# A gated long convolution and SwiGLU block: split norm statistics, a last stage in 64-row pairs, two spectra kept in SBUF, and a third weight buffer

## Chip, cores and metric

The kernel runs on one core of a Trainium2 chip. The metric is the device time of one execution in microseconds (us), the median of five runs. The profiler records a single execution, whose span is counted from its first to its last recorded work; that execution's own time is given beside it.

## What is computed

One block of an adaLN-conditioned model on a sequence of 2048 rows of width 576, in bf16. Six rows `sa, ca, ga, sb, cb, gb` come from a condition vector. The first half is a gated long convolution, the second half a SwiGLU of width 4608:

```python
h = _layernorm(x) * (1 + ca) + sa
# k_shift: 4-tap causal filter over the rows of k
kv = k_shift * v
y = irfft(rfft(kv, 2 * S) * rfft(ssm_k, 2 * S))[:S] + kv * ssm_D
x = x + ga * (h * y)
h = _layernorm(x) * (1 + cb) + sb
x = x + gb * ((silu(h @ w1) * (h @ w3)) @ w2)
```

## The kernel before

**Blocks.** The convolution is done over 8 blocks of 256 rows (`s` = 0 to 7). Each block of `kv` has a spectrum `X[s]` and each block of the filter has a spectrum `W[s]`, from which `V[s]` is made of two neighbours; both are [128, 6, 576] bf16, 0.885 MB. Block s of the result is the sum over j of `X[j] * V[s - j]` (`pair`, L400 to L412: two VectorE operations, a product and a sum, per term), put back by `inverse` (L539, TensorE), and joined to x in `residual` (L552 to L554, VectorE). Spectra that later blocks need are written to HBM by `keep_x` (L417) and `keep_v` (L421) and read back by `get` (L433) into `spec`, a pool of three buffers for X and four for V; `old_x` and `old_v` say which are still in SBUF.

**Statistics.** A norm's sums are made by ScalarE (`ln_sums`, L440: a copy and a square with an accumulated output). `ln_scales` (L455 to L460) makes mean, variance, `pow(var, -0.5)` and the shift of them in six GpSimd operations on 128x2 values. For the first norm the result is used by `gate_rows` (L500, ScalarE, tile `hg`), for the second by `normed_act` (L566, ScalarE, tile `h2row`). Block 0 and 1 use VectorE's batch-norm instructions in part (`quick_stats`, L470 to L473).

**Turns.** `turn_all(s)` transposes `h2row` on TensorE (L571), and ScalarE writes it scaled to `h2T` (L601), the input of the SwiGLU.

**Stages.** `row_blocks` runs four stages r of 512 rows. `stream` makes the hidden rows of 36 chunks ("items") of 128 columns. An item fills two PSUM banks, one for w1 and one for w3. As 576 is 4.5 times 128, each bank gets four full 128-row matmuls (`full`, L916, 128x512) and one of 64 rows (`rest`, L927); the two half ones of an item lie in the upper and lower half of the array. Items go in groups of 2, in the last stage of 4: the full ones of the early items, then all half ones, then the full ones of the late items. `hide` then applies Silu (L935) and copies the second bank (L937) on ScalarE and multiplies on VectorE (L938). `down` (L982) multiplies with w2: two halves of 288 columns, each with 144 matmuls of 128x288 and 9 w2 chunks loaded by SyncE, evicted at L999 and L1000.

**What sets the order.** The convolution of blocks 2r+2 and 2r+3 (`conv`, `outcome`, generators that yield a cost in us) is threaded through stage r: after each item and each w2 chunk `advance` runs steps until a budget is spent. The amounts are `CONV_US` over a time of 93.5 us. `behind(engine)` pins an instruction's place behind the last one already issued on that engine. `first_block` does block 0 in a hand-written order, `conv_second` block 1. The last stage has no convolution beside it. In `down`, at half 1, chunk 5, what is left of the convolution is run off and `turn_all(2r + 3)` issued. All weight and spectra transfers are issued by SyncE in program order.

**Weight buffers.** `wst` has three buffers of [128, 9, 512]. `load_w13` (L867, L868) brings a chunk of w1 and w3 (four items, 1.15 MB) into one of them. From stage 1 on, chunks alternate between buffers 0 and 1; `wst[2]` then serves `down` as four w2 buffers (`w2m`). Two lines of it, from `row_blocks` and `down`:

```python
jobs = [(fc, 0, RB, (r + fc) % 2, ...) for fc in range(NF // FC)]
w = _ap(self.w2m, (h * NF + f0) // W2C % NW2 * W2C * H, [[H, W2C], [1, H]])
```

Of the kernel before, what the change touches and what calls it, by code (L numbers as in the profile page):

```python
# [9 lines left out]
BF16 = mybir.dt.bfloat16  # L10
F32 = mybir.dt.float32
I32 = mybir.dt.int32
ALU = mybir.AluOpType
ACT = mybir.ActivationFunctionType

P = 128
# [16 lines left out]
N1 = 24  # L33
SPLIT = 2
EPS = 1e-5

# [7 lines left out]
class _Kernel:  # L44
    def __init__(self, ctx, tc, q, k, v, shift_k, ssm_k, ssm_D, w1, w3, w2, c, w_mod, out):
        self.tc, self.nc = tc, tc.nc
        self.q, self.k, self.v = q, k, v
        self.shift_k, self.ssm_k, self.ssm_D = shift_k, ssm_k, ssm_D
        self.w1, self.w3, self.w2, self.c, self.w_mod, self.out = w1, w3, w2, c, w_mod, out
        pool = lambda name, **kw: ctx.enter_context(tc.tile_pool(name=name, **kw))  # L50
        self.const = pool("const", bufs=1)
        self.psum = pool("psum", bufs=4, space=bass.MemoryType.PSUM)
        self.dram = pool("spill", bufs=1, space=bass.MemoryType.DRAM)
        self.spec = pool("spec", bufs=4)
        self.wprev = pool("wprev", bufs=2)
        self.prod = pool("prod", bufs=1)
        self.acc = pool("acc", bufs=1)
        self.ld = pool("ld", bufs=1)
        self.kvp = pool("kvp", bufs=1)
        self.x1p = pool("x1p", bufs=4)  # L60
        self.lnp = pool("lnp", bufs=1)
        self.small = pool("small", bufs=4)
        self.hp = pool("hp", bufs=4)
        self.xo, self.hg, self.accs, self.l1 = {}, {}, {}, {}
        self.X, self.V, self.Wl = {}, {}, {}
        self.w13, self.kept = {}, {}

    def ps(self, shape=(P, 2, 512), dtype=F32):
# [280 lines left out]
    def x_sums(self, s):  # L349
        X = self.X[s]  # L350
        self.nc.vector.tensor_add(X[:, 0:6:3, :], X[:, 1:6:3, :], X[:, 2:6:3, :])
        if 3 < s < NBLK - 2:
            self.keep_x(s)
        yield 0.75
# [68 lines left out]
    def old_x(self, i, s):  # L423

        return self.X[i] if s == 2 or s == 4 and i > 0 else self.get("X", i)

# [9 lines left out]
    def ln_sums(self, src, i, ssum, ssq, col=None):  # L436
        col = i if col is None else col
        for func, out in ((ACT.Copy, ssum), (ACT.Square, ssq)):
            junk = self.lnp.tile([P, D], BF16, name="junk", tag="junk")
            self.nc.scalar.activation(junk[:], src[:, i, :], func, accum_out=out[:, col:col + 1])  # L440

    def ln_stats(self, src, name):

        ssum = self.small.tile([P, 2], F32, name=name + "s", tag="ssum")
        ssq = self.small.tile([P, 2], F32, name=name + "q", tag="ssq")
        for i in range(2):
            self.ln_sums(src, i, ssum, ssq)
        return self.ln_scales(ssum, ssq, name)

    def ln_scales(self, ssum, ssq, name):  # L450
        small = self.small
        n = ssum.shape[-1]
        mean, var, rstd, nmr = [small.tile([P, n], F32, name=name + k, tag=f"ln{k}{n}") for k in "mvrn"]
        e = self.nc.gpsimd
        e.tensor_single_scalar(mean[:], ssum[:], -1.0 / D, op=ALU.mult)  # L455
        e.tensor_scalar(var[:], ssq[:], 1.0 / D, EPS, op0=ALU.mult, op1=ALU.add)
        e.tensor_mul(rstd[:], mean[:], mean[:])
        e.tensor_sub(var[:], var[:], rstd[:])
        e.tensor_tensor(rstd[:], var[:], self.neghalf[:, 0:n], op=ALU.pow)
        e.tensor_mul(nmr[:], mean[:], rstd[:])  # L460
        return rstd, nmr
# [22 lines left out]
    def gate_stats(self, s):  # L484

        ssum, ssq = [self.small.tile([P, 2], F32, name="l1" + k, tag=t) for k, t in (("s", "ssum"), ("q", "ssq"))]
        for i in range(2):
            with self.behind(self.nc.scalar):
                self.ln_sums(self.xo[s], i, ssum, ssq)
            yield 0.8  # L490
        self.l1[s] = self.ln_scales(ssum, ssq, "l1")

# [68 lines left out]

    def normed_act(self, s, r, b):
        row, x1 = self.h2row, self.xo[s]
        for cc in range(2):
            for lo, hi, at in ((0, D, 0), (512, D, D)):
# [62 lines left out]
    def first_block(self):  # L628
# [54 lines left out]
        self.ln_sums(x1, 0, sums[0], sums[1], 0)  # L683
        scales = [self.ln_scales(*sums, "l1"), (rstd, nmr)]
        for m in (1, 0):
# [50 lines left out]
    def outcome(self, s, fill, waits, between=None, quick=False):  # L736


        def steps():
# [19 lines left out]
            else:  # L759
                with self.behind(nc.scalar):  # L760
                    r, b = self.ln_stats(self.xo[s], "l2")
                yield -waits[2]
                with self.behind(nc.scalar):
                    self.normed_act(s, r, b)
            yield -waits[3]
# [11 lines left out]
    def conv_second(self):  # L777
        yield from self.gate_stats(1)
        yield from self.kv_rows(1)
        yield from self.v_block(1)  # L780
        yield from self.pair(self.X[0], self.V[1], 1)
        yield from self.x_spectrum(1)
        self.mod_piece(5)
# [9 lines left out]
    def conv(self, s0):  # L793
# [13 lines left out]
        def old():  # L807
            V, X = self.old_v(s0 - 1, s0), self.old_x(1, s0)
            yield from self.pair(X, V, s0)
            for j in range(2, s0):  # L810
                X = self.old_x(j, s0)
                yield from self.pair(X, V, s1)
                V = self.old_v(s0 - j, s0)
                yield from self.pair(X, V, s0)
            self.V1 = V
            yield from self.gate_stats(s0)
            yield from self.kv_rows(s0)
            if s0 == 2:
                yield from self.pair(self.X[0], self.V[s0], s0)
        yield from self.mix(filters(), old())  # L820
        self.gate_rows(s0)
        X0, V0 = self.old_x(0, s0), self.old_v(0, s0)

        def beside():
            yield from self.v_block(s1)
            with self.behind(self.nc.sync):
                self.load_kv(s1)
            yield from self.gate_stats(s1)
            if s0 > 2:
                yield from self.pair(X0, self.V[s0], s0)  # L830
            self.X1 = self.old_x(1, s0)
            yield from self.pair(X0, self.V[s1], s1)
            yield from self.gate(s0)
        yield from self.mix(self.x_spectrum(s0), beside())
# [7 lines left out]
        def others():  # L842
            yield from self.kv_rows(s1)
            yield from self.mix(self.x_spectrum(s1), more())
            yield from self.x_sums(s1)
# [35 lines left out]
    def stream(self, r, jobs, rate, size, finish=False):  # L881
# [49 lines left out]
        def hide(k):  # L931
# [7 lines left out]
            del gus[k]  # L939
            self.advance(rate * 2.05)  # L940

# [4 lines left out]
        for k in range(0, len(items), size):  # L946
# [13 lines left out]
            for m in late:  # L960
                full(m, False)
                hide(m)

    def down(self, r, rate):
# [71 lines left out]
    def row_blocks(self, n1):  # L1036
        for r in range(NRB):
# [17 lines left out]
            else:  # L1055
                spills = {1: (self.keep_x, 1), 2: (self.keep_v, 0), 4: (self.keep_v, 1)} if r == 1 else {}
                jobs = [(fc, 0, RB, (r + fc) % 2, (lambda f, i: lambda: f(i))(*spills[fc]) if fc in spills else None)
                        for fc in range(NF // FC)]
            self.stream(r, jobs, rate, 4 if r == NRB - 1 else 2)
            self.down(r, rate)  # L1060
# [54 lines left out]
```

## Time and profile before

| | |
|---|---|
| five runs, us | 517.81, 518.19, 518.25, 518.63, 519.36 |
| median | 518.25 |
| profiled execution, its own time | 518.19 |
| its span | 516.1 |
| TensorE matmul busy | 498.1 us, 97% |
| VectorE, ScalarE, GpSimd busy | 341.2, 292.8, 63.6 us |
| moved by DMA | 107.76 MB, 209 GB/s |
| L916, full matmuls | 1317 records, 263.7 us |
| L927, half matmuls | 336, 42.4 us |
| L982, `down` | 1152, 145.3 us |
| Xd written, read | 6 and 8 transfers of 864 KB |
| Vd written, read | 4 and 4 |

In the groups a line gives the code line, the engine, the operation and its tiles as output<-input, then the count, the busy time and the mean of one in ns. Durations of matmuls overlap, as they are pipelined; the distance from start to start is what counts. In the timeline a bracket holds the idle time of the engine ahead of a group and what ended it. In the chain, lines give start, length, engine, tile and line. The stages, by the first matmuls of each: stage 0 up to 163 us, stage 1 to 283, stage 2 to 399, the last from there to the end. The page's "PEclk" is the clock that TensorE was granted, in tenths of full speed.

### The profile page before, as it was taken

The numbers are of one execution on the slowest core, as the hardware profiler recorded it, in microseconds if no ns is written. First come the engines' busy times: TensorE is split into PE (matmuls) and PEld (weight loads), VectorE is DVE, ScalarE is ACT, GpSimd is POOL, SyncE is SP. The second block draws the span as 40 slices with busy tenths as digits, with TensorE's granted clock in tenths as the row PEclk, the third lists the DMA queues.
The fourth block names the chain that finished last, engine by engine and source line by source line (L and its number), as shares of the span: only waits on it lengthen the run. The fifth ranks groups of instructions, "written<-read, shape, count | busy, mean of one in ns | idle before, by whom it ended". The sixth has DMA issues, their size and how long they took to land.

```text
span 516.1 us, 8602 instructions
## 1 busy us (share of the span) xinstructions
PE 498.1 (97%) x3334; PEld 294.3 (57%) x3362; DVE 341.2 (66%) x515; ACT 292.8 (57%) x581; POOL 63.6 (12%) x109
## 2 busy tenths in 40 slices
PE   7999988999999999999998999999999999999997
PEld 3767763556787444344776543434588544444775
DVE  8899898999994364997999984299660212112012
ACT  5758697578443569659552465976806345445000
POOL 3303013104040001201017000120101000000000
PEclk9989998999999999999999999999999999999999
DMA  8947968587979857559999863645555553550462
GB/s 274 323 150 217 321 197 253 161 287 240 294 250 343 262 185 217 185 157 322 343 321 353 286 190 127 188 158 169 151 139 139 148 173 121 162 168 10 118 181 70
DMA packets 102204, 107.76 MB, mean 209 GB/s; under 512 B 5075, under 2 KB 94228, under 8 KB 102164
## 3 DMA queue, kind: packets, MB, share of 16 engines
q1 hardware_dynamic: 102142, 107.21, 66.5%
q8 instruction: 26, 0.43, 0.4%
q14 instruction: 14, 0.11, 0.1%
q10 hardware_dynamic: 22, 0.01, 0.0%
HBM read 96.00 MB, written 11.21 MB: 208 GB/s over the span
## 4 chain that ended last, share of the span: by engine, by line
PE 76%; DVE 13%; DMA 4%; ACT 3%; issue 2%; POOL 2%; SPq 0%; POOLq 0%; ACTq 0%
PE ps L916 38%; PE ps L982 24%; PE ps L927 6%; DMA wst<-in_B_w_dram 3%; DVE p L410 2%; PE ps L313 2%; PE ps L299 2%; PE ps L539 2%; DVE z L412 2%; DVE h L938 1%; DVE kv L335 1%; DVE kvt L334 1%; DMA knat<-in_A_ssm_k_dram 1%; PE ps L219 1%; PE ps L364 1%
## 5 line engine op out<-in xcount | busy, mean ns | idle before, releaser
L916 PE MATMUL ps<-h2T,wst 128*128 128x512 bf16 (+1 forms) x1317 | 263.7, 350 | 2.8 <-ACT W L315 0.8
L916 PEld LDWEIGHTS <-wst 128*128 128x128 bf16 x1344 | 127.9, 98 | 122.3 <-issue 19.5
L935 ACT ACTIVATE h<-ps 128x512 bf16<-128x512 f32 x144 | 87.0, 604 | 108.4 <-PE ps L927 70.8
L982 PE MATMUL ps<-wst,h 128*128 128x288 bf16 x1152 | 145.3, 286 | 3.1 <-DMA wst<-in_B_w_dram 2.4
L982 PEld LDWEIGHTS <-h 128*128 128x128 bf16 x1152 | 112.3, 98 | 32.7 <-issue 3.9
L938 DVE TENSOR_TENSOR h<-h,u 128x512 bf16<-128x512 bf16 x144 | 60.1, 420 | 96.1 <-ACT u L937 95.9
L937 ACT CAST u<-ps 128x512 bf16<-128x512 f32 x144 | 84.9, 590 | 0.0
L410 DVE TENSOR_TENSOR p<-X,V 128x3456 bf16<-128x3456 bf16 x28 | 54.6, 1949 | 5.7 <-DMA X<-Xd 5.5
L412 DVE TENSOR_TENSOR z<-z,p 128x3456 bf16<-128x3456 bf16 x28 | 54.6, 1950 | 0.2
L999 DVE TENSOR_TENSOR og<-ps,gbrow 128x288 bf16<-128x288 f32 x32 | 13.1, 448 | 48.9 <-PE ps L982 48.9
L927 PE MATMUL ps<-h2T,wst 64*128 64x512 bf16 (+1 forms) x336 | 42.4, 349 | 2.4 <-ACT X L315 2.1
L440 ACT ACTIVATE junk<-x 128x576 bf16<-128x576 bf16 x54 | 37.6, 696 | 0.5
L927 PEld LDWEIGHTS <-wst 64*128 64x128 bf16 x336 | 11.4, 94 | 29.4 <-issue 26.6
L455 POOL TENSOR_SCALAR l2m<-l2s 128x2 f32<-128x2 f32 x6 | 8.8, 1469 | 154.4 <-ACT junk L440 154.4
L601 ACT ACTIVATE h2T<-ps,sbcol,cbcol 128x256 bf16<-128x256 bf16 x35 | 16.7, 570 | 17.6 <-PE ps L571 17.6
L566 ACT ACTIVATE h2row<-x,l2n,l2r 128x576 bf16<-128x576 bf16 (+1 forms) x24 | 13.8, 654 | 21.2 <-POOL l2n L460 21.2
L455 POOL TENSOR_SCALAR l1m<-l1s 128x2 f32<-128x2 f32 x7 | 4.4, 634 | 131.6 <-ACT junk L440 131.6
L334 DVE TENSOR_TENSOR kvt<-kh,shk 128x1152 bf16<-128x1152 bf16 x24 | 18.0, 750 | 2.6 <-DMA kh<-in_A_k_dram 2.4
L335 DVE TENSOR_TENSOR kv<-kv,kvt 128x1152 bf16<-128x1152 bf16 x24 | 18.0, 752 | 0.3
L315 ACT CAST X<-ps 128x576 bf16<-128x576 f32 x24 | 15.5, 658 | 0.0
L745 ACT CAST y<-ps 128x576 bf16<-128x576 f32 x14 | 8.6, 653 | 11.1 <-PE ps L539 11.1
L405 DVE TENSOR_TENSOR z<-X,V 128x3456 bf16<-128x3456 bf16 x7 | 13.6, 1949 | 0.9 <-PE ps L927 0.9
(137 smaller groups left out, 370.2 us busy)
## 6 DMA issues: line engine op xcount, KB each, us to landing
wst<-in_B_w_dram SPq DMA_DIRECT2D x80, 512.0 KB, 4.8
wst<-in_B_w_dram SPq DMA_DIRECT2D x72, 288.0 KB, 3.8
X<-Xd SPq DMA_DIRECT2D x8, 864.0 KB, 5.5
Xd<-X SPq DMA_DIRECT2D x6, 864.0 KB, 5.9
wst<-in_B_w_dram SPq DMA_DIRECT2D x80, 64.0 KB, 3.0
kh<-in_A_k_dram SPq DMA_DIRECT2D x7, 720.0 KB, 7.7
Vd<-V SPq DMA_DIRECT2D x4, 864.0 KB
V<-Vd SPq DMA_DIRECT2D x4, 864.0 KB
```

Source lines behind the costliest of these rows:

```text
L334: nc.vector.tensor_mul(tmp[:], kh[:, 3 - j:5 - j, :], tap(j))
L335: nc.vector.tensor_add(kv[:], kv[:], tmp[:])
L410: nc.vector.tensor_mul(p[:], X[:], V[:])
L412: nc.vector.tensor_add(z[:], z[:], p[:])
L440: self.nc.scalar.activation(junk[:], src[:, i, :], func, accum_out=out[:, col:col + 1])
L601: nc.scalar.activation(dst, src, ACT.Identity, bias=self.sbcol[:, ct:ct + 1], scale=self.cbcol[:, ct:ct + 1])
L916: nc.tensor.matmul(gus[k][:, i, a * n:(a + 1) * n], w[:, 5 * i + ct, (fi + a) * P:(fi + a + 1) * P], hT[:, ct, t0:t1], start=(first and ct ...
L927: nc.tensor.matmul(gus[k][:, i, a * n:(a + 1) * n], w[rows, 4, (fi + a) * P:(fi + a + 1) * P], hT[rows, 4, t0:t1], start=(first and a == 0 ...
L935: nc.scalar.activation(h3, gus[k][:, 0, :].rearrange("p (a t) -> p a t", a=m), ACT.Silu)
L937: nc.scalar.copy(u[:], gus[k][:, 1, :])
L938: nc.vector.tensor_mul(h3, h3, u[:].rearrange("p (a t) -> p a t", a=m))
L982: nc.tensor.matmul(acc[t], self.h3[:, f0 + f, t * P:(t + 1) * P], w[:, f, :], start=(f0 + f == 0), stop=(f0 + f == NF - 1))
```

## The change

1. **Statistics.** ScalarE's accumulated outputs are scaled (by -1/D and D^-0.5), so that they are the negative mean and the mean square. `ln_scales` is split into `ln_var` (two VectorE operations, then `pow` on GpSimd) and `ln_shift` (one VectorE operation). In block 0 the same are on GpSimd. They are placed as steps of their own (`gate_var`, `gate_shift`), and `gate_rows` stands later in `conv`; in `outcome` the second norm's sums, variance, shift and rows are separate steps with waits between.
2. **Last stage.** `stream_halves` takes the place of `stream` for r = 3: each item is nine pairs of 64-row matmuls. The first pass writes rows 0 to 63 of all five row tiles to one bank and rows 64 to 127 to the other, the second pass (four row tiles) with banks swapped. Between the passes of an item stand the first two pairs (`AHEAD`) of the next item, and the second pass waits for the last matmul of the first.
3. **Spectra.** X4 and X5 are not written to HBM and not read back. For blocks 6 and 7 the loop of products keeps X falling and V rising, so Xd has 4 writes and 5 reads and Vd 4 writes and 5 reads.
4. **Third buffer.** From stage 1 on, the chunks of w1 and w3 go through buffers 0, 1, 2, 0, 1, 2, 0, 1, 0 (0 and 1 exchanged in odd stages); buffer 2 still serves w2 in `down`.
5. **Head.** In the first 8 items of stage 1, `advance` gets 1.4 times the budget.

The diff, with unchanged parts left out:

```diff
 SPLIT = 2
+HEAD = 8
+HEAD_PACE = 1.4
+AHEAD = 2
 EPS = 1e-5
...
         self.w13, self.kept = {}, {}
+    def newest(self):
+        return self.nc.cur_bb.bb.instructions[-1]
+    def after(self, first):
+        with self.behind(self.nc.tensor):
+            nop = self.nc.tensor.nop().ins
+            self.tc.add_manual_dep(
+                nop, first.name,
+                mybir.DependencyInfo(mybir.DependencyClass.Sync, mybir.DependencyReason.DATA),
+                reason="both halves of the rows write this bank, one after the other")
+        return self.tc.issue_after(nop)
...
         self.nc.vector.tensor_add(X[:, 0:6:3, :], X[:, 1:6:3, :], X[:, 2:6:3, :])
-        if 3 < s < NBLK - 2:
-            self.keep_x(s)
         yield 0.75
...
-        return self.X[i] if s == 2 or s == 4 and i > 0 else self.get("X", i)
+        return self.X[i] if s == 2 or s == 4 and i > 0 or i >= 4 else self.get("X", i)
...
         col = i if col is None else col
-        for func, out in ((ACT.Copy, ssum), (ACT.Square, ssq)):
+        for func, scale, out in ((ACT.Copy, -1.0 / D, ssum), (ACT.Square, D ** -0.5, ssq)):
             junk = self.lnp.tile([P, D], BF16, name="junk", tag="junk")
-            self.nc.scalar.activation(junk[:], src[:, i, :], func, accum_out=out[:, col:col + 1])
-    def ln_scales(self, ssum, ssq, name):
-        small = self.small
+            self.nc.scalar.activation(junk[:], src[:, i, :], func, scale=scale, accum_out=out[:, col:col + 1])
+    def ln_var(self, ssum, ssq, name, engine=None):
         n = ssum.shape[-1]
-        mean, var, rstd, nmr = [small.tile([P, n], F32, name=name + k, tag=f"ln{k}{n}") for k in "mvrn"]
-        e = self.nc.gpsimd
-        e.tensor_single_scalar(mean[:], ssum[:], -1.0 / D, op=ALU.mult)
-        e.tensor_scalar(var[:], ssq[:], 1.0 / D, EPS, op0=ALU.mult, op1=ALU.add)
-        e.tensor_mul(rstd[:], mean[:], mean[:])
-        e.tensor_sub(var[:], var[:], rstd[:])
-        e.tensor_tensor(rstd[:], var[:], self.neghalf[:, 0:n], op=ALU.pow)
-        e.tensor_mul(nmr[:], mean[:], rstd[:])
+        var, rstd = [self.small.tile([P, n], F32, name=name + k, tag=f"ln{k}{n}") for k in "vr"]
+        e = engine or self.nc.vector
+        e.tensor_mul(var[:], ssum[:], ssum[:])
+        if engine is None:
+            e.scalar_tensor_tensor(var[:], ssq[:], EPS, var[:], op0=ALU.add, op1=ALU.subtract)
+        else:
+            e.tensor_sub(var[:], ssq[:], var[:])
+            e.tensor_single_scalar(var[:], var[:], EPS, op=ALU.add)
+        self.nc.gpsimd.tensor_tensor(rstd[:], var[:], self.neghalf[:, 0:n], op=ALU.pow)
+        return ssum, rstd, name
+    def ln_shift(self, ssum, rstd, name, engine=None):
+        n = ssum.shape[-1]
+        nmr = self.small.tile([P, n], F32, name=name + "n", tag=f"lnn{n}")
+        (engine or self.nc.vector).tensor_mul(nmr[:], ssum[:], rstd[:])
         return rstd, nmr
...
             yield 0.8
-        self.l1[s] = self.ln_scales(ssum, ssq, "l1")
+        self.l1[s] = ssum, ssq, "l1"
+    def gate_var(self, s):
+        self.l1[s] = self.ln_var(*self.l1[s])
+    def gate_shift(self, s):
+        self.l1[s] = self.ln_shift(*self.l1[s])
...
-    def normed_act(self, s, r, b):
+    def normed_act(self, s, cc, r, b):
         row, x1 = self.h2row, self.xo[s]
-        for cc in range(2):
+        with self.behind(self.nc.scalar):
             for lo, hi, at in ((0, D, 0), (512, D, D)):
...
         self.ln_sums(x1, 0, sums[0], sums[1], 0)
-        scales = [self.ln_scales(*sums, "l1"), (rstd, nmr)]
+        scales = [self.ln_shift(*self.ln_var(*sums, "l1", nc.gpsimd), nc.gpsimd), (rstd, nmr)]
         for m in (1, 0):
...
             else:
-                with self.behind(nc.scalar):
-                    r, b = self.ln_stats(self.xo[s], "l2")
-                yield -waits[2]
-                with self.behind(nc.scalar):
-                    self.normed_act(s, r, b)
+                sums = [self.small.tile([P, 2], F32, name="l2" + k, tag=t) for k, t in (("s", "ssum"), ("q", "ssq"))]
+                for i in range(2):
+                    with self.behind(nc.scalar):
+                        self.ln_sums(self.xo[s], i, *sums)
+                    yield 0.0
+                yield -waits[2] / 2
+                stats = self.ln_var(*sums, "l2")
+                yield -waits[2] / 2
+                scales = self.ln_shift(*stats)
+                yield -3.0
+                for cc in range(2):
+                    self.normed_act(s, cc, *scales)
+                    yield -1.0
             yield -waits[3]
...
         yield from self.v_block(1)
+        self.gate_var(1)
         yield from self.pair(self.X[0], self.V[1], 1)
+        self.gate_shift(1)
         yield from self.x_spectrum(1)
...
         def old():
-            V, X = self.old_v(s0 - 1, s0), self.old_x(1, s0)
-            yield from self.pair(X, V, s0)
-            for j in range(2, s0):
-                X = self.old_x(j, s0)
-                yield from self.pair(X, V, s1)
-                V = self.old_v(s0 - j, s0)
+            if s0 < NBLK - 2:
+                V, X = self.old_v(s0 - 1, s0), self.old_x(1, s0)
                 yield from self.pair(X, V, s0)
-            self.V1 = V
+                for j in range(2, s0):
+                    X = self.old_x(j, s0)
+                    yield from self.pair(X, V, s1)
+                    V = self.old_v(s0 - j, s0)
+                    yield from self.pair(X, V, s0)
+                self.V1 = V
+            else:
+                V, X = self.old_v(1, s0), self.old_x(s0 - 1, s0)
+                yield from self.pair(X, V, s0)
+                for j in range(2, s0):
+                    V = self.old_v(j, s0)
+                    yield from self.pair(X, V, s1)
+                    X = self.old_x(s0 - j, s0)
+                    yield from self.pair(X, V, s0)
+                self.X1 = X
             yield from self.gate_stats(s0)
             yield from self.kv_rows(s0)
+            self.gate_var(s0)
             if s0 == 2:
...
         yield from self.mix(filters(), old())
-        self.gate_rows(s0)
         X0, V0 = self.old_x(0, s0), self.old_v(0, s0)
...
             yield from self.v_block(s1)
+            self.gate_shift(s0)
             with self.behind(self.nc.sync):
...
                 yield from self.pair(X0, self.V[s0], s0)
-            self.X1 = self.old_x(1, s0)
+            if s0 < NBLK - 2:
+                self.X1 = self.old_x(1, s0)
+            else:
+                self.V1 = self.old_v(1, s0)
+            self.gate_rows(s0)
             yield from self.pair(X0, self.V[s1], s1)
+            self.gate_var(s1)
             yield from self.gate(s0)
...
             yield from self.kv_rows(s1)
+            self.gate_shift(s1)
             yield from self.mix(self.x_spectrum(s1), more())
...
             del gus[k]
-            self.advance(rate * 2.05)
+            self.advance(rate * 2.05 * (HEAD_PACE if r == 1 and k < HEAD else 1.0))
...
+    def stream_halves(self, r, jobs):
+        nc = self.nc
+        hT = self.h2T[r % 2]
+        items = [(job, fi) for job in jobs for fi in range(FC)]
+        gus, ws = {}, {}
+        def part(k, swap, some=slice(None)):
+            (fc, _, _, _, _), fi = items[k]
+            cols = slice(fi * P, (fi + 1) * P)
+            order = (0, 1, 2, 3) if swap else (4, 0, 1, 2, 3)
+            for ct in order[some]:
+                for rows, i in ((slice(0, 64), swap), (slice(64, P), 1 - swap)):
+                    nc.tensor.matmul(gus[k][:, i, :], ws[fc][rows, 5 * i + ct if ct < 4 else 4, cols], hT[rows, ct, :],
+                                     start=swap == 0 and ct == 4, stop=swap == 1 and ct == 3)
+            return self.newest()
+        def begin(k):
+            if k == len(items):
+                return
+            (fc, _, _, buf, also), fi = items[k]
+            if fi == 0:
+                if fc not in self.w13:
+                    self.load_w13(fc, buf)
+                ws[fc] = self.w13.pop(fc)
+                if also is not None:
+                    with self.behind(nc.sync):
+                        also()
+            gus[k] = self.ps()
+            part(k, 0, slice(0, AHEAD))
+        def hide(k):
+            (fc, _, _, _, _), fi = items[k]
+            h3 = self.h3[:, fc * FC + fi, :]
+            nc.scalar.activation(h3, gus[k][:, 0, :], ACT.Silu)
+            u = self.hp.tile([P, RB], BF16, name="u", tag="u")
+            nc.scalar.copy(u[:], gus.pop(k)[:, 1, :])
+            nc.vector.tensor_mul(h3, h3, u[:])
+        begin(0)
+        for k in range(len(items)):
+            mark = part(k, 0, slice(AHEAD, None))
+            begin(k + 1)
+            with self.after(mark):
+                part(k, 1)
+            hide(k)
     def down(self, r, rate):
...
                 spills = {1: (self.keep_x, 1), 2: (self.keep_v, 0), 4: (self.keep_v, 1)} if r == 1 else {}
-                jobs = [(fc, 0, RB, (r + fc) % 2, (lambda f, i: lambda: f(i))(*spills[fc]) if fc in spills else None)
+                bufs = [b if b == 2 else (r + b) % 2 for b in (0, 1, 2, 0, 1, 2, 0, 1, 0)]
+                jobs = [(fc, 0, RB, bufs[fc], (lambda f, i: lambda: f(i))(*spills[fc]) if fc in spills else None)
                         for fc in range(NF // FC)]
-            self.stream(r, jobs, rate, 4 if r == NRB - 1 else 2)
+            if r == NRB - 1:
+                self.stream_halves(r, jobs)
+            else:
+                self.stream(r, jobs, rate, 2)
             self.down(r, rate)
...
```

## The prediction on record

> **What bounds the kernel now.** I read, in this order, the page's busy times and clock slices, the windows by stage, the chain in order of time, the waits, and the timeline at TensorE's gaps. From the page:
>
> ```profile
> PE 498.1 (97%) x3334; PEld 294.3 (57%) x3362; DVE 341.2 (66%) x515; ACT 292.8 (57%) x581; POOL 63.6 (12%) x109
> ...
> PEclk9989998999999999999999999999999999999999
> ```
>
> The windows of the four stages (length; busy PE, PEld, DVE, ACT, POOL; clock; DMA share; GB/s):
>
> ```profile
> 34.00:163.00 129.00, 122.97 (x995) 86.41 (x999) 117.71 (x162) 85.99 (x173) 26.20 (x32) 0.99 0.78 242
> 163.00:282.60 119.60, 117.19 (x727) 63.48 (x733) 93.75 (x125) 73.53 (x147) 18.31 (x24) 1.00 0.81 265
> 282.60:399.10 116.50, 115.31 (x715) 62.55 (x721) 77.78 (x106) 71.10 (x144) 8.81 (x24) 1.00 0.57 175
> 399.10:516.00 116.90, 112.58 (x692) 63.02 (x696) 22.72 (x60) 40.19 (x77) 0.00 (x0) 0.99 0.44 127
> ```
>
> TensorE is the bound everywhere. Only what it waits for, or pays between matmuls, can be saved: about 6 us in stage 0, where VectorE is nearly full as well, and 1 to 4 us in each later stage. Where it waits, from the waits and the timeline:
>
> ```profile
> ACT hg L500 <- POOL l1n L460: 2.9, 1, 2.9
> PE ps L982 <- DMA wst<-in_B_w_dram: 2.4, 3, 1.6
> ```
>
> ```profile
> 83.63 0.39 PE L927 MATMUL ps<-h2T,wst 64*128 64x512 bf16 x2 [2.15 <-ACT X L315]
> 148.91 3.96 POOL L455 TENSOR_SCALAR l2m<-l2s 128x2 f32<-128x2 f32 x1 [24.59 <-ACT junk L440]
> 155.18 2.29 ACT L566 ACTIVATE h2row<-x,l2n,l2r 128x576 bf16<-128x576 bf16 x4 [5.54 <-POOL l2n L460]
> 161.60 0.72 PE L571 MATMUL ps<-ident,h2row 128*128 128x128 bf16 x10
> 272.44 7.91 POOL L460 TENSOR_TENSOR l2n<-l2m,l2r 128x2 f32<-128x2 f32 x1
> 386.24 0.72 PE L571 MATMUL ps<-ident,h2row 128*128 128x128 bf16 x10
> 394.12 2.29 ACT L566 ACTIVATE h2row<-x,l2n,l2r 128x576 bf16<-128x576 bf16 x4 [1.66 <-POOL l2n L460]
> 398.55 0.72 PE L571 MATMUL ps<-ident,h2row 128*128 128x128 bf16 x10
> ```
>
> At 81 us TensorE stands 2.15 us, since the spectrum's eviction is queued on ScalarE behind `hg`, which waits for GpSimd's statistics. Three waits for w2 come to 2.4 us: some 0.5 after the turn at 161.60, 0.31 and 1.56 at 272 to 276. The chain shows the last stage's rhythm:
>
> ```profile
> 309.03 3.56 PE ps L916 x16
> 313.12 3.56 PE ps L916 x16
> ...
> 408.61 0.97 PE ps L927 x8
> 416.59 0.97 PE ps L927 x8
> ```
>
> **What the Trainium skill says.** "TensorEngine Tiling (Array Packing)", Key Properties: a change of tiling mode drains TensorE. The chain agrees, priced below at 0.21 us for a change and back. The same page, Gotcha 1 (PSUM Pressure): different row tiles can't use one PSUM bank at once; no run here shows that, but it is why the new stage needs its wait. "SBUF — State Buffer", "two separate sides": VectorE and GpSimd lock a shared port pair for a whole instruction. The trace fits: `l2n` takes 7.91 us at 272.44 where its like at 393.90 takes 0.20. "TensorE: Matmul & The Clock Gate", Part 1: an idle window of about 3.4 us halves the clock. Here the gap at 81 us is followed by 3.4 us at clock 0.50 (84.4 to 87.8), and the 1.56 us gap at 274 by nothing.
>
> **Last stage in 64-row pairs.** Stages 1 and 2 take 4.095 us per two items (309.03 to 313.12): 18 slots x and two mode changes. The last stage takes 7.98 us per four items (408.61 to 416.59): 36 x and two changes. Doubling the first and subtracting, two changes cost 0.21 us and x = (7.98 − 0.21)/36 = 0.216 us, for a full matmul and for a pair of half ones alike. After, an item has 9 pairs where it had 8 full matmuls and a pair: 9 slots either way. Nine groups paid 9 × 0.21 = 1.89 us. The new order has two entries and exits (one `down` matmul stands ahead of the last eight half matmuls): 0.42. Gain 1.5 us. The added wait on TensorE's own count holds all that is queued on TensorE, and so the whole stage. It stands behind two pairs of the next item; at that distance such a load already waits in the old trace, and the next pair starts 0.655 us after the matmul waited for, three slots, so nothing is lost. Bounds: 0, or a slot an item (36 × 0.216 = 7.8 us) if the wait were a slot longer; I take 0. Its 576 more weight loads of 0.094 us (L927's row) lie two to a 0.216 slot. If they didn't hide, the stage would lose up to 324 slots × some 0.01 us; the gain would be gone at 0.005 a slot. Four consecutive pairs at 0.216 speak against it.
>
> **Split statistics.** Each of 13 block statistics had six GpSimd operations; now one (`pow`, 0.72 undisturbed, at most 1.26) stays, and three small ones go to VectorE. The page has none of their shape; the nearest rows are L471's 0.147 (128x1) and L470's 0.202 (128x2), and I take 0.15: 5.9 us more VectorE work, of which some 2 in stage 0. The 2.9 us wait of `hg` goes, and with `gate_rows` placed later the stall at 81 us, since X evictions no longer stand behind it. So TensorE is freed of 2.15 us, the half clock's 1.7, and 0.7 at inverse(3): about 4.5 us. What is late next? Turn(3), whose place among TensorE's instructions is unchanged. It needs VectorE's residual of block 3, the new variance steps, `pow`, the shift and ScalarE's rows. VectorE has no idle time from 104 to 137 us, and there waits in order for three `pow` round trips (two of block 2's and 3's gate, one of block 2's second norm; behind each stand the spectra's products and the next kv rows, and behind those TensorE) of 0.85 (the longest sum I can build from a 0.72 `pow`), against 1.9 us of its old idle time that goes. I put residual(3) at 147.2 (before 145.7). The built order sets about 10 us of other VectorE work between it and the variance: 157.2; two small operations, `pow`, a running product and the shift add 2.4, the rows 2.3: 161.9, against 161.60. So the freed 4.5 us is mostly waited off at the turn: +0.3. The w2 wait behind it (0.5) goes, as TensorE stood longer. A gap of 3 to 4 us may halve the clock: 1.7 us at one chance in four, 0.4. **Stage 0: +0.2**, bounds −2.9 and +3.6.
>
> **Stage 1.** X4 and X5 stay in SBUF: two spill writes and two reads fewer, 4 × 0.885 = 3.5 MB. In stage 1's `down` five spectra loads stand between w2 loads where seven did. DMA there is at 370 to 390 GB/s with a share over 1.0, so w2 comes late for want of DMA time. The two waits (1.87) and a 0.3 us gap at turn(5) can go; I take **−1.8**, bounds −2.5 and 0. Turn(5) has about 6 us of slack in the new order, and there `pow` replaces an operation that was locked out for 7.91.
>
> **Third buffer, head pace.** No work is added. The first four w2 loads now wait for chunk 5's matmuls: three chunks of 8.2 us cover a landing of 3.8. Chunk 2's load waits for the previous `down`: 16 us ahead of use against a landing of 4.8. Cost 0; if that cover were gone, up to 4.8 us a stage. `HEAD_PACE` moves conv work 2 to 4 us earlier on TensorE, and adds none: 0, bounds −0.5 and +0.5, as VectorE has 26 us free in this stage but is full in part of it. `hg`, moved later, is 0.85 us of ScalarE either way.
>
> **Stage 2.** In the new order, inverse(7) stands 48 `down` matmuls (5.9 us) later and turn(6) 32 (4.0), turn(7) where it was, leaving 64 matmuls of 0.1225 between the turns instead of 96: with the turn itself 8.6 us. The chain from turn(6) to turn(7)'s input was 394.12 + 2.29 − 386.24 = 10.2, and is 0.3 shorter with fewer operations: 9.9. **+1.3**, bounds 0 (the sums run ahead of the turn) and +2.
>
> **Sum.** +0.2 − 1.8 + 1.3 − 1.5 = −1.8 us, against the profiled execution's 518.19 (its span 516.1 and 2.1 around it): 516.4. That execution is 0.06 under the median, so no correction.
>
> **Rivals.** A: VectorE reaches turn(3) in time, and the freed 2.15 and 0.73 us are kept: −2.9 in place of +0.2, 513.3. For it: `pow` no longer stands behind five others, and the evictions come earlier. Against: the full VectorE row. C: w2 still comes late, because the third buffer draws the next w1 and w3 loads into the same stretch and takes the freed DMA time: 1.8 back, 518.2. For it: the DMA share is above 1.0 through 265 to 275. Against: fewer loads in between. D, slower: VectorE now stands in its queue for GpSimd. Four round trips in stage 0 at 1.4 instead of 0.85 (the longest `pow`, 1.26, and its hops) are 2.2 us later at turn(3), and the longer gap brings the half clock in full, 1.7 instead of 0.4: 516.4 + 3.5 = 519.9. It decides from the point where turn(3) starts later than about 165. Against: a VectorE that waits holds no port.
>
> **How the numbers follow.** The likeliest case: 45%, own range 515.4 to 517.4. A 25%, C 17%, D 13%. The range 513.0 to 519.0 leaves out the lower end of A and most of D. About 0.2% (1.0 us) is what a measurement of this kernel can tell from no change. Under 517.2: most of the likeliest (0.39), A and a little of C: 0.66. Above 519.3: 0.12. Between: 0.22.
>
> **What would show it.** Right: no 8 us rhythm in the last stage, nine pairs in 1.94 us; no gap at 81 us and no half clock there; turn(3) near 161.6 with a TensorE gap ahead of it; `down` of stage 1 without DMA waits; a 1 us gap ahead of turn(7). Wrong: pairs above 0.22 us; turn(3) 3 us earlier or 3 later; new waits at w1 or w3.

## The result, and the profile after

The changed kernel takes 520.78 us (median of 23 runs) against 518.2 before (44 runs): 1.0042 of the time, 95% interval 1.0027 to 1.0057. It is slower, by 2.6 us at the medians, where 516.4 was forecast. Times here and below leave out executions that took over 1.5% more than the fastest one of the same kernel (one of the changed kernel, three of gate_split_only, one each of gpsimd_no_spectra_no_buffer and head_undone). The profiled execution took 522.56, which is 1.8 above the median; its span is 520.8. From its page:

```profile
PE 501.2 (96%) x3630; PEld 297.1 (57%) x3650; DVE 345.1 (66%) x554; ACT 293.9 (56%) x581; POOL 23.7 (5%) x43
...
PEclk9979999979999999999999999999999999999999
```

GpSimd's work fell from 63.6 to 23.7 us, VectorE's grew by 3.9 (5.9 were forecast), and the clock's dips are deeper, the second of them now in the ninth slice instead of the seventh. The timeline at the places that the prediction named (its line numbers are those of the new file: L557 is `inverse`, L572 `residual`, L589 a turn, L1073 `down`, L1090 its eviction, L1022 the new last stage):

```profile
88.65 0.15 DVE L460 TENSOR_TENSOR l1v<-l1s 128x2 f32<-128x2 f32 x1
89.06 0.15 DVE L462 SCALAR_TENSOR_TENSOR l1v<-l1q,l1v 128x2 f32<-128x2 f32 x1
89.29 0.69 POOL L466 TENSOR_TENSOR l1r<-l1v,neghalf 128x2 f32<-128x2 f32 x1 [8.76 <-DVE l1v L462]
90.02 0.16 DVE L472 TENSOR_TENSOR l1n<-l1s,l1r 128x2 f32<-128x2 f32 x1 [0.81 <-POOL l1r L466]
104.22 1.12 PE L557 MATMUL ps<-z,Fb 128*128 128x288 bf16 x4 [2.90 <-DVE z L543]
149.81 0.75 DVE L572 TENSOR_TENSOR x<-x,hg 128x1152 bf16<-128x1152 bf16 x1
154.56 10.65 PE L1073 MATMUL ps<-wst,h 128*128 128x288 bf16 x72 [2.00 <-DVE og L1090]
161.62 2.29 ACT L584 ACTIVATE h2row<-x,l2n,l2r 128x576 bf16<-128x576 bf16 x4 [5.02 <-DVE l2n L472]
166.51 0.72 PE L589 MATMUL ps<-ident,h2row 128*128 128x128 bf16 x10
404.13 0.56 PE L589 MATMUL ps<-ident,h2row 128*128 128x128 bf16 x5 [0.53 <-ACT h2row L584]
```

The waits of the changed kernel (in all, times, longest) say how often VectorE stood:

```profile
DVE l2v L460 <- ACT junk L454: 8.4, 2, 6.9
DVE l1n L472 <- POOL l1r L466: 4.8, 7, 0.9
DVE l2n L472 <- POOL l2r L466: 3.6, 5, 0.9
PE ps L557 <- DVE z L543: 2.9, 1, 2.9
```

The stand at 81 us is gone. In its place TensorE stands 2.90 us at block 2's inverse transform and 2.00 us at the start of `down`'s second half, both times for VectorE. Each is followed by a stretch at half clock (windows of the changed kernel; columns as before):

```profile
103.70:110.50 6.80, 6.06 (x30) 3.58 (x32) 6.80 (x9) 1.28 (x2) 0.00 (x0) 0.50 0.30 103
154.90:158.30 3.40, 3.40 (x17) 2.13 (x15) 3.40 (x8) 1.63 (x5) 0.00 (x0) 0.50 0.34 106
```

The same by stages, from turn to turn on TensorE, each from one profiled execution (us):

| kernel | turn 1 to 3 | 3 to 5 | 5 to 7 | 7 to last `down` matmul | half clock in it |
|---|---|---|---|---|---|
| before | 97.4 | 120.4 | 116.6 | 113.5 | 3.4 |
| changed | 101.5 | 118.1 | 118.4 | 112.9 | 10.2 |
| halves_only | 97.4 | 120.3 | 116.7 | 112.1 | 3.4 |
| no_stats | 97.3 | 120.7 | 116.3 | 112.0 | 3.4 |
| vector_late_shift | 97.1 | 118.7 | 117.4 | 112.9 | 3.4 |
| gpsimd_new_places | 96.3 | 117.6 | 118.0 | 112.9 | 0 |
| gpsimd_norm2_whole_67 | 95.9 | 117.6 | 117.1 | 112.0 | 0 |

So the changed kernel loses 4.1 us in stage 0 and 1.8 in stage 2, and gains 2.3 in stage 1. Its last stage is dealt with below. The table leaves out the start up to turn(1) and the end behind the last matmul; each is 0.8 us longer in this execution than in that of the kernel before. Nothing here tells whether the change has a part in that.

### The profile page after: what moved, and what is told of

Read it like the earlier page. It is cut to its first block, busy times and chain, and to the rows that moved or that the text cites. A ratio compares the mean times of both kernels' runs of the same rounds, so it can differ in the third digit from the quotient of the medians.

```text
span 520.8 us, 9161 instructions
## 1 busy us (share of the span) xinstructions
PE 501.2 (96%) x3630; PEld 297.1 (57%) x3650; DVE 345.1 (66%) x554; ACT 293.9 (56%) x581; POOL 23.7 (5%) x43
## 4 chain that ended last, share of the span: by engine, by line
PE 64%; DVE 23%; ACT 8%; issue 2%; DMA 1%; POOL 1%; POOLq 0%; SPq 0%; ACTq 0%; DVEq 0%
PE ps L961 24%; PE ps L1073 17%; PE ps L1022 13%; DVE p L424 5%; DVE z L426 4%; PE ps L972 4%; ACT junk L454 2%; PE ps L329 2%; DVE h L983 2%; PE ps L557 1%; DVE kv L351 1%; DVE kvt L350 1%; DMA V<-Vd 1%; DVE z L419 1%; ACT u L982 1%
## 5 line engine op out<-in xcount | busy, mean ns | idle before, releaser
L961 PE MATMUL ps<-h2T,wst 128*128 128x512 bf16 (+1 forms) x1037 | 200.4, 342 | 2.2 <-ACT W L331 0.8
L961 PEld LDWEIGHTS <-wst 128*128 128x128 bf16 x1056 | 100.9, 99 | 87.6 <-issue 15.1
L1073 PE MATMUL ps<-wst,h 128*128 128x288 bf16 x1152 | 147.3, 288 | 3.1 <-DVE og L1090 2.0
L1073 PEld LDWEIGHTS <-h 128*128 128x128 bf16 x1152 | 113.0, 98 | 33.8 <-issue 4.5
L1022 PE MATMUL ps<-h2T,wst 64*128 64x512 bf16 x648 | 70.3, 376 | 0.0
L1022 PEld LDWEIGHTS <-wst 64*128 64x128 bf16 x648 | 31.3, 94 | 38.3 <-issue 0.2
L1090 DVE TENSOR_TENSOR og<-ps,gbrow 128x288 bf16<-128x288 f32 x32 | 13.2, 449 | 41.8 <-PE ps L1073 41.8
L972 PE MATMUL ps<-h2T,wst 64*128 64x512 bf16 (+1 forms) x264 | 33.1, 344 | 0.3
L972 PEld LDWEIGHTS <-wst 64*128 64x128 bf16 x264 | 8.6, 95 | 21.3 <-issue 19.7
```

What stands on the lines that cost most here:

```text
L961: nc.tensor.matmul(gus[k][:, i, a * n:(a + 1) * n], w[:, 5 * i + ct, (fi + a) * P:(fi + a + 1) * P], hT[:, ct, t0:t1], start=(first and ct ...
L972: nc.tensor.matmul(gus[k][:, i, a * n:(a + 1) * n], w[rows, 4, (fi + a) * P:(fi + a + 1) * P], hT[rows, 4, t0:t1], start=(first and a == 0 ...
L1022: nc.tensor.matmul(gus[k][:, i, :], ws[fc][rows, 5 * i + ct if ct < 4 else 4, cols], hT[rows, ct, :], start=swap == 0 and ct == 4, stop=sw ...
L1073: nc.tensor.matmul(acc[t], self.h3[:, f0 + f, t * P:(t + 1) * P], w[:, f, :], start=(f0 + f == 0), stop=(f0 + f == NF - 1))
```

## The experiments

All times are medians; the ratio is to the kernel before as it was timed beside each run, with its 95% interval. Of each edit the main lines are shown; `...` marks what is left out.

| kernel | us | ratio |
|---|---|---|
| halves_only | 517.23 | 0.9981 (0.9969 to 0.9992) |
| stats_only | 521.36 | 1.0065 (1.0041 to 1.0090) |
| no_stats | 516.16 | 0.9956 (0.9936 to 0.9976) |
| fill_inverse2 | 520.61 | 1.0042 (1.0026 to 1.0058) |
| gate_split_only | 519.45 | 1.0025 (1.0004 to 1.0046) |
| norm2_split_only | 516.24 | 0.9962 (0.9943 to 0.9982) |
| gpsimd_new_places | 515.76 | 0.9940 (0.9918 to 0.9962) |
| vector_old_places | 522.49 | 1.0078 (1.0054 to 1.0101) |
| gpsimd_plus_vector_load | 518.87 | 1.0004 (0.9984 to 1.0025) |
| vector_late_shift | 516.04 | 0.9959 (0.9937 to 0.9981) |
| gpsimd_norm2_whole_67 | 513.62 | 0.9899 (0.9878 to 0.9919) |
| gpsimd_no_spectra_no_buffer | 519.40 | 1.0007 (0.9987 to 1.0027) |
| kept_undone | 514.08 | 0.9921 (0.9895 to 0.9947) |
| third_undone | 513.69 | 0.9915 (0.9889 to 0.9941) |
| head_undone | 516.98 | 0.9981 (0.9961 to 1.0000) |

**Which part: halves_only, stats_only, no_stats.** The first two put one part of the change on the kernel before, the third takes the statistics out of the changed kernel.

```diff
# halves_only, on the kernel before
...
-            self.stream(r, jobs, rate, 4 if r == NRB - 1 else 2)
+            if r == NRB - 1:
+                self.stream_halves(r, jobs)
+            else:
+                self.stream(r, jobs, rate, 2)
# no_stats, on the changed kernel
-        self.l1[s] = ssum, ssq, "l1"
+        self.l1[s] = self.ln_scales(ssum, ssq, "l1")
...
+        self.gate_rows(s0)
         X0, V0 = self.old_x(0, s0), self.old_v(0, s0)
```

> The kernel before with the last stage in 64-row pairs and nothing else of the change. If mode changes were the whole cost of the last stage's rhythm, it gains 1.5 us (516.7 us against 518.2), all behind 400 us of the span, and stages 0 to 2 stay. If weight loads or the wait between the passes bound the pairs, the stage keeps its length or grows: 518.2 or more.

> The kernel before with the split statistics and their new places alone; spectra, buffers, head pace and last stage as before. Theory (TensorE, freed at 81 us, runs into VectorE's later results in gaps over 2 us, and each such gap halves the clock for 3.4 us or twice that): slower, 520.5 to 524, with half-clock stretches at about 104 and 155 us. Rival (spectra order or third buffer make the loss in stages 0 and 2): within 0.5 us of 518.2, no such gaps.

> The changed kernel with the statistics as before (six GpSimd operations, hg in its old place). Theory: stage 0 goes back to the old one, the last stage's 1.5 us and the 2.2 us of w2 waits stay gained: 514.5, up to 517 if the 2.8 us that stage 2 lost belong to the order of the products. Rival (buffers, spectra or head pace at fault): 519 to 521.

halves_only gained 1.0 us by the ratio, and 1.4 where the stage table isolates it. The statistics alone cost 3.4 us, and the changed kernel without them gains 2.3 on the kernel before. The loss is theirs. (The profile of stats_only has the first of the two half-clock stretches that were expected, at 104.8 us, and not the second.) But stage 1 of no_stats is as long as before, and its w2 waits are 2.5 us in all, where they were 2.4. So what the changed kernel wins in stage 1 doesn't come from the saved transfers by themselves: that half of the expectation missed.

**Is it the clock? fill_inverse2.** Matmuls whose result is not used keep TensorE busy ahead of inverse(2).

```diff
             terms = [(3 * cc, 1, cc), (3 * cc, 0, 3 - cc)]
+        for _ in range(22 if (s, cc) == (2, 0) else 0):
+            nc.tensor.matmul(ps[:, 0, 0:H], self.ident[:], self.h2T[0][:, 0, 0:H], start=True, stop=True)
```

> The changed kernel with 22 matmuls of 128x288 whose result is not used (2.7 us of TensorE work) put ahead of block 2's inverse transform, so that TensorE is busy where it stood 2.9 us. Theory (the gap's price is the clock): the half clock at 104 to 110 us goes, the time of inverse(2) itself stays, and the kernel is 1.5 to 3 us faster than the changed one: 518 to 519. Rival (VectorE is late by itself, and the clock only goes along): 520.8 as without it.

In the profile the half clock at 104 us did go, and the median did not follow: 520.61. TensorE now stands 0.85 us for `kv` at 107 us and 2.22 at the start of `down`'s second half, and the half clock came there (151.7). In this file L559 is `inverse`, L329 the transform of `kv` and L1075 `down`:

```profile
102.68 0.65 PE L559 MATMUL ps<-z,Fb 128*128 128x288 bf16 x4
107.90 0.66 PE L329 MATMUL ps<-kv,Fb 128*128 128x288 bf16 x4 [0.85 <-DVE kv L353]
151.90 4.29 PE L1075 MATMUL ps<-wst,h 128*128 128x288 bf16 x21 [2.22 <-DVE og L1092]
```

inverse(2) starts 39.1 us behind turn(1), as in the changed kernel (39.2), so VectorE was late by itself. The theory that the clock is the whole price falls. That the clock adds to it isn't excluded: the intervals of the two ratios are each 0.3% (1.6 us) wide, so a gain of up to 1 us or so would not show.

**Place or engine, gate or second norm.** Two theories stood: the new places of the steps, or VectorE standing in its queue.

```diff
# gate_split_only: second norm in one piece on GpSimd
-                stats = self.ln_var(*sums, "l2") ... scales = self.ln_shift(*stats) ...
+                scales = self.ln_shift(*self.ln_var(*sums, "l2", nc.gpsimd), nc.gpsimd)
...
# norm2_split_only: gate in one piece on GpSimd, hg in its old place
+        self.l1[s] = self.ln_shift(*self.ln_var(ssum, ssq, "l1", self.nc.gpsimd), self.nc.gpsimd)
...
# gpsimd_new_places: all on GpSimd, steps where the change has them
-        e = engine or self.nc.vector
+        e = engine = self.nc.gpsimd
...
# vector_old_places: both norms on VectorE and pow, in one piece where the old ones stood
+        self.l1[s] = self.ln_shift(*self.ln_var(ssum, ssq, "l1"))
...
```

> The changed kernel with the second norm's statistics back in one piece on GpSimd (five operations right behind the sums, rows after one wait); the gate's statistics stay split on VectorE and in their new places. Theory 1 (the second norm's separate steps set when inverse transforms and turns come on TensorE, and that order is what loses 2.8 us in stage 2 and part of stage 0): 516 to 517, near the kernel without the split. Theory 2 (VectorE stands in its queue for pow at the gates): 519 to 520.

> The changed kernel with the gate's statistics back in one piece on GpSimd and hg in its old place; the second norm stays split with its separate steps. TensorE's order is that of the changed kernel, instruction for instruction. Theory 1: slow as the changed kernel, 519.5 to 521. Theory 2: 516 to 517.5. If the stall at 81 us, which comes back here, is what kept TensorE from running into VectorE, stage 0 is as long as before and only stage 2's 2.8 us remain: 519.

> The changed kernel with all statistics operations on GpSimd (five per norm), in the changed kernel's places and with its TensorE order. Theory 1 (places): 519.5 to 521.5, stage 2 loses the same 2.8 us. Theory 2 (VectorE as the engine): 516 to 517.5.

> The changed kernel with the statistics split onto VectorE and GpSimd's pow as in the change, but run in one piece where the old ones stood, hg and the second norm's rows in their old places. Theory 1: 515.5 to 517. Theory 2: 519 to 521, with VectorE standing for pow in each norm.

All four went the way of theory 2, two of them by some 0.2 and 1.5 us outside the numbers given. VectorE as the engine of the gate's statistics is the loss, in either place; in the old places it is larger, and the profile adds a stand of 2.8 us at 41 us and w2 waits in stage 1 there. The second norm on VectorE costs little. The places by themselves cost nothing: 515.76 with the changed kernel's TensorE order, against 516.16 for no_stats. By the stage table they give 3.1 us in stage 1 and take most of it back in stage 2 and at turn(7).

**The standing or the operations: vector_late_shift, gpsimd_plus_vector_load.** The first moves the gate's shift behind later VectorE operations, so that VectorE doesn't stand for `pow`. The second adds two unused products at each of the two gates that stand ahead of inverse(2).

```diff
# vector_late_shift, on the changed kernel
+        with self.behind(self.nc.vector):
-        self.l1[s] = self.ln_shift(*self.l1[s])
+            self.l1[s] = self.ln_shift(*self.l1[s])     # called right ahead of gate_rows
...
# gpsimd_plus_vector_load, on gpsimd_new_places, in gate_var for s in (2, 3)
+            with self.behind(self.nc.vector):
+                for _ in range(2):
+                    self.nc.vector.tensor_mul(p[:, 0:2, :], a, b)
```

> The kernel with all statistics on GpSimd in the new places (515.8 us), with two VectorE products whose result is not used (128x1152, 0.67 us each from start to start) put where the gate's variance of blocks 2 and of 3 stood on VectorE: 2.7 us of VectorE work, about what the split's operations and their two waits for pow took ahead of inverse(2). Theory 2 (VectorE's time ahead of inverse(2) is the price, whatever fills it): TensorE stands some 3 us at inverse(2) again, the half clock comes back in many executions, 518.5 to 520. Rival (pow, or the statistics' own chain): 515.5 to 516.5.

> The changed kernel with the gate's shift put behind later VectorE operations, so that VectorE does not stand for pow at the gates; operations and TensorE order are unchanged. Theory 2, if the standing (0.81 us at a gate, two of them ahead of inverse(2)) is most of it: the gap at inverse(2) falls from 2.9 to about 1.3 us, 518 to 519. If the small operations themselves are most of it: 520 to 521.

The wait at inverse(2) in three timelines: gpsimd_new_places, vector_late_shift, gpsimd_plus_vector_load.

```profile
102.23 0.65 PE L557 MATMUL ps<-z,Fb 128*128 128x288 bf16 x4 [0.73 <-ACT h L980]
```

```profile
100.82 0.65 PE L558 MATMUL ps<-z,Fb 128*128 128x288 bf16 x4 [1.25 <-ACT u L982]
```

```profile
105.99 0.65 PE L564 MATMUL ps<-z,Fb 128*128 128x288 bf16 x4 [3.27 <-DVE z L550]
```

With no VectorE statistics 0.73 us, with the operations but no standing 1.25, with both 2.90 (the changed kernel), with plain products in their place 3.27. From 2.90 to 1.25 is 1.65, twice 0.81. In the first two the profile names ScalarE as the last to come; VectorE's `z` was ready within 0.1 us of it, so what is left there isn't VectorE's alone. vector_late_shift gains 4.7 us on the changed kernel by the medians (4.3 by the ratios), more than expected: the stand for the eviction shrinks as well, from 2.00 to 1.22 us, and there is less half clock (3.4 us against 10.2 in the stage table). The loaded kernel loses 3.1 on its base. VectorE's time ahead of inverse(2) is the cause, whatever fills it. How much of the loss each later meeting adds is not shown: in its profile the loaded kernel is 1.6 us longer between turns 1 and 3, and as much between turns 3 and 5, where it waits 1.49 us for w2.

**Stage 2: gpsimd_norm2_whole_67.**

```diff
+                if s > 5:
+                    with self.behind(nc.scalar):
+                        ...sums of both rows...
+                        scales = self.ln_shift(*self.ln_var(*sums, "l2"))
+                    yield -waits[2]
+                    for cc in range(2):
+                        self.normed_act(s, cc, *scales)
```

> All statistics on GpSimd in the new places, but for blocks 6 and 7 the second norm in one piece with one wait, as before the change. If the second norm's separate steps cost stage 2 its 1.3 to 2.6 us (a wait at turn(7), at the second inverse and at the eviction ahead of it): 513 to 514.5. If that loss has another source: 515.8.

Turn(7) in gpsimd_new_places and in this kernel:

```profile
396.79 0.56 PE L589 MATMUL ps<-ident,h2row 128*128 128x128 bf16 x5 [0.35 <-ACT h2row L584]
397.88 0.56 PE L589 MATMUL ps<-ident,h2row 128*128 128x128 bf16 x5 [0.53 <-ACT h2row L584]
```

```profile
394.13 0.72 PE L589 MATMUL ps<-ident,h2row 128*128 128x128 bf16 x10
```

It hit: the separate steps of the second norm cost about 2 us from turn(5) on (0.9 up to turn(7), 0.9 behind it by the stage table). At 513.62 this is the fastest kernel, 1.0% under the one before.

**Parts 3 to 5.** First all three undone on gpsimd_new_places, then each alone on the fastest kernel.

> All statistics on GpSimd in the new places and the last stage in pairs, but spectra of blocks 4 and 5 spilled and read back, two w1/w3 buffers and head pace 1.0 as before the change. If the transfers saved and the third buffer are what lets w2 come in time in stage 1: w2 waits of 2 us come back, 517 to 518. If TensorE's new order does that: 515.5 to 516.3.

> The fastest kernel so far (513.6 us: GpSimd statistics, second norm of blocks 6 and 7 whole) with the spectra of blocks 4 and 5 spilled and read back and the old loop of products; TensorE's order is unchanged. If the saved transfers are what makes stage 1 shorter (the prediction's step): w2 waits of about 2 us in stage 1 come back, 515.5 to 516.5. If they lie beside TensorE's work: 513.6.

> The same kernel with two w1/w3 buffers instead of three; TensorE's and VectorE's orders are unchanged. The prediction's price for the third buffer was 0: 513.6. If w1/w3 loaded earlier free the queue for spectra and w2: 515 to 517.

> The same kernel with head pace 1.0 in stage 1. The prediction's price for it was 0: 513.6. If it is what brings turn(5)'s rows in time (a wait of 4.8 us there was seen with all three parts undone): 516 to 518.

```diff
# kept_undone: keep_x(4), keep_x(5) and the old loop of products back
+        if 3 < s < NBLK - 2:
+            self.keep_x(s)
...
# third_undone
-                bufs = [b if b == 2 else (r + b) % 2 for b in (0, 1, 2, 0, 1, 2, 0, 1, 0)]
+                bufs = [(r + b) % 2 for b in range(9)]
# head_undone
-HEAD_PACE = 1.4
+HEAD_PACE = 1.0
```

Undone together they cost 3.6 us by the medians, more than expected. The timeline of that kernel's profiled execution, which took 521.80, shows where:

```profile
254.19 4.08 PE L1075 MATMUL ps<-wst,h 128*128 128x288 bf16 x32 [1.94 <-DMA wst<-in_B_w_dram]
283.20 0.56 PE L591 MATMUL ps<-ident,h2row 128*128 128x128 bf16 x5 [4.60 <-ACT h2row L586]
```

Undone alone, the head pace costs 3.4 us by the medians (4.2 by the ratios). The spectra and the third buffer cost 0.5 and 0.1 by the medians (1.1 and 0.8 by the ratios), and their intervals overlap that of the kernel that has them, so an effect of theirs on the whole time is not shown. In head_undone inverse(5) stands at 259.1 us instead of 253.0 and turn(4) at 266.8 instead of 260.8. VectorE's last products of the stage are then late at the eviction behind it, and the half clock follows at 288.7:

```profile
288.55 1.08 PE L378 MATMUL ps<-ident,knat 128*128 128x128 bf16 x10 [1.94 <-DVE og L1100]
```

## Why the prediction was wrong

- **Last stage, −1.5: right.** The rhythm is gone, and pairs go through without a stop: 320 of them in the 69.18 us from 410.50 to 479.68, 0.216 each. Between the matmuls behind turn(7) (399.11 before, 404.53 after) and the first eviction of the last half (510.88 and 514.81) the new stage is 5.42 − 3.93 = 1.49 us shorter. Nothing bound the pairs or the wait between passes:

```profile
410.50 69.24 PE L1022 MATMUL ps<-h2T,wst 64*128 64x512 bf16 x640
479.68 0.30 PE L1073 MATMUL ps<-wst,h 128*128 128x288 bf16 x1
479.91 1.04 PE L1022 MATMUL ps<-h2T,wst 64*128 64x512 bf16 x8
480.88 5.32 PE L1073 MATMUL ps<-wst,h 128*128 128x288 bf16 x42
```

- **Stage 0, +0.2: the step that failed,** measured +4.1 in the profiled execution. The round trip was priced rightly (0.85; the stands are 0.81, 0.81 and 0.80). What failed is "What is late next? Turn(3)". I followed VectorE's lateness to the turn and passed over two meetings on the way: inverse(2), which TensorE now reached 3 us earlier and VectorE 1.3 later, and the eviction that frees `down`'s accumulators. The prediction put residual(3) at 147.2; it ended at 150.5 (of these 3.3 us, 0.8 were there at turn(1) already, and 0.9 are two waits of VectorE for ScalarE at 111 and 122 us; the rest isn't taken apart). The rows of turn(3) were ready at 163.9 instead of 161.9, and turn(3) came at 166.5, as TensorE had stood at 152 us and run at half clock to 158.3.
- **The half clock, 0.4: mis-sized.** I gave one stretch one chance in four; the profiled execution has three between turns 1 and 3, 5.1 us of lost clock against 1.7 before. The prediction counted one gap of 3 to 4 us; two gaps of 2.0 and 2.9 did it. The half-clock time of an execution can be worked out as twice the missing share of its granted clock times its span. Over 24 executions of the changed kernel it is 11.0 us in the mean (6.7 in 50 of the kernel before), and a straight line through the 24 gives 0.33 us of time for 1 us of it. Some 1.4 of the 2.6 us would be accounted for that way, but by correlation only: in fill_inverse2 the mean is 7.3, and the median is 0.2 us below the changed kernel's where the line would have 1.2.
- **Rival D** had the cause, VectorE standing for GpSimd, and the side. Its price was built on longer round trips, which did not come, and on turn(3) as its place, where the meeting was not.
- **Stage 1, −1.8: the size near (−2.3), partly by luck, as the reason given does not do it alone.** The w2 waits did fall, to 0.4 us in the changed kernel. But they stayed in no_stats, which has all of parts 3 to 5, and came back in part in kept_undone, the fastest kernel without the saved transfers. Changed kernel, no_stats, kept_undone:

```profile
PE ps L1073 <- DMA wst<-in_B_w_dram: 0.4, 1, 0.4
PE ps L1055 <- DMA wst<-in_B_w_dram: 2.5, 3, 1.0
PE ps L1085 <- DMA wst<-in_B_w_dram: 1.1, 2, 1.0
```

Stage 1 is short (117.6 us) in gpsimd_new_places and long (120.7) in no_stats, so the new places, with the order of TensorE that they give, are needed. In single profiles, kept_undone takes 119.2 there and norm2_split_only, with the new order and the transfers saved, 119.5 with a w2 wait of 1.8. So neither the order nor the transfers settle it, and their shares are not shown.

- **Stage 2, +1.3: right in sign, half in size,** measured +1.8, with 0.9 of turn(7)'s wait counted behind it, so about 2.7 in all. Only these 0.9 lie at turn(7), where the prediction had all of it. Besides, there are waits of 0.69 for the eviction at 294 us, 0.95 for `y` at inverse(6) and 0.74 for ScalarE's `u` at 373, which the prediction didn't see; the first two were not there before.
- **Third buffer at 0: right** as far as the runs tell. **Head pace at 0, bounds 0.5: wrong by 3.4 us** in the fastest kernel; it was not undone alone in the changed one. "Adds no work" was true, but a step that comes 6 us earlier is worth what it spares at the next meeting.

## What to carry to other kernels

When a wait is removed, follow the engine that is freed to every point where it meets the one that is nearly full, in order, and not only to the last one: here the first such meeting took the freed time back. In this kernel a short chain across engines was better off on the engine with room, or with its last link behind other work: 0.8 us of standing on a full in-order engine was paid at each of two gates. Test engine and place apart; here the new places cost nothing and the new engine lost.

## What the runs showed of the hardware

Two stands of TensorE of 2.0 and 2.9 us were each followed by half clock, for 3.4 and for 6.8 us: one gap can cost two such stretches. The Trainium skill, "TensorE: Matmul & The Clock Gate", Part 1, speaks of an idle window of about 3.4 us; here a stand of 2.0 us in a busy stretch was enough, and in the kernel before one of 1.56 was not. But the length of a stand doesn't decide it alone. In vector_late_shift 1.25 us (with one of 0.69 close behind) was followed by half clock; in gpsimd_plus_vector_load 3.27 us was not. Windows behind the two stands, in this order:

```profile
102.50:105.90 3.40, 3.40 (x18) 2.31 (x17) 3.40 (x5) 0.64 (x1) 0.00 (x0) 0.50 0.30 106
106.00:116.00 10.00, 9.28 (x69) 5.77 (x71) 10.00 (x12) 5.73 (x11) 0.00 (x0) 1.00 0.36 122
```

In each trace the clock's changes up to the last matmul lie whole multiples of 3.41 us apart (in the changed kernel the two stretches begin at 103.69 and 154.89, 15 multiples). So what may count is how a stand lies in that rhythm; no run tests it.

How much half clock comes differs from execution to execution of one kernel (3 to 21 us over 24 of the changed one), and the changed kernel's times spread more: 517.3 to 523.8 in all but one of 24 runs, 512.6 to 514.4 in 5, which are few, of the fastest kernel, which has no stand above 1.5 us from turn(1) to its last matmul.

A pair of 64-row matmuls kept the 0.216 us of a full one through a whole stage, with two weight loads of 0.094 us in each.
